# Forming the remainders of double-precision weights on GpSimd instead of TensorE, in an attention and gated-MLP kernel

## The chip, the cores and the metric

The kernel runs on one core of a Trainium2 chip. The core has TensorE (PE in the profile, with its weight loads as PEld), VectorE (DVE), ScalarE (ACT), GpSimd (POOL) and SyncE (SP), which here issues all DMAs. TensorE's results land in PSUM, a memory of eight banks of 128 x 512 float32. The metric is the device time of one execution in microseconds (us), as the median of several runs on the chip.

## The reference

Eight batches, eight heads, 576 tokens, heads of 64. The attention keeps only the scores within `tau` of a row's maximum. Its output, with the heads side by side (512 wide), goes through a gated MLP with a residual.

```python
def _attn_ref(q, k, v, tau):
    scores = scale * np.matmul(q, k.transpose(0, 1, 3, 2))
    thresh = np.max(scores, axis=-1, keepdims=True) - tau
    scores = np.where(scores >= thresh, scores, -1000000000.0)
    scores = scores - np.max(scores, axis=-1, keepdims=True)
    attn = np.exp(scores)
    attn = attn / (np.sum(attn, axis=-1, keepdims=True) + 1e-09)
    return np.matmul(attn, v)

def _moe_ref(x, w_in, g_ln, w_sg, b_sg, w_out):
    h = gelu_tanh(x @ w_in)                              # 512 -> 1024
    u, v = (h[..., :d_ff // 2], h[..., d_ff // 2:])
    v_n = (v - mean(v)) / np.sqrt(var(v) + 1e-06) * g_ln
    v_s = np.einsum('ts,bsd->btd', w_sg, v_n) + b_sg[None, :, None]
    return x + (u * v_s) @ w_out
```

`w_in` (512 x 1024) and `w_out` (512 x 512) arrive in double precision, all else in float32.

## The kernel before

**Two streams of work.** The attention works on 32 pairs of heads, n = 0 to 31, four to a batch. Each pair has nine score tiles of 128 x 576: TensorE forms the scores (L525, L537 for n < 4; L545 after that), DVE takes their maximum (L554), GpSimd a threshold from it (L560, one column), ACT the exponential (L581), and DVE selects, multiplies and sums (L588). For n < 4 the scores are float32 products and the selected tiles are transposed on TensorE (L250) before the product with the values (L727). From n = 4 on, queries and keys are split into two float32r parts (high and low, so that a float32 product becomes two or three float32r products), and DVE turns 32 x 32 blocks (L603) for many small products with the values (L741). The MLP of a batch (`moe`, its products in groups of four at L839) begins when its four pairs are done. Its operands are float32r pairs too: `xh`, `xl` of the attention's output, `wih`, `wil` of `w_in`, `woh`, `wol` of `w_out`.

**The weights** are prepared once, during the first pairs, by `from_double` (L278 to L332). `w_in` makes eight jobs of 128 x 512 ("wide", k = 0 to 7), `w_out` eight jobs of 128 x 256 ("narrow", k = 14 to 21). A job loads the doubles as two 32-bit words, ACT takes the magnitude of the upper word (L293), GpSimd clamps it (L302), and three DVE steps on bits rebuild it as a float32 number in the tile `room` (L308, L310, L312); the last one leaves the scale of the lower word in place of the upper one. The low word is scaled on GpSimd in wide jobs (L297), on ACT in narrow ones (L299). ACT rounds `room` to float32r: that is the high part, `hi` (L329). The low part is `room - hi` plus the low word times its scale. GpSimd forms that last product (L315). TensorE adds the three in a bank of PSUM (L321): `room` times the identity as a float32 product, `hi` times minus the identity (held in the tile `zt1`) and the low word's term times the identity as float32r products. ACT copies the bank into `lo` (L332).

**What sets the order.** Nothing is scheduled at run time and no planner runs at build time. Each step of work is put on a list, and the table `ORDER`, packed into a string, gives the sequence in which the steps are issued (L1150). Each engine takes its own instructions in that sequence and waits by semaphores for what it needs. A second table, `FIRST_BANKS`, gives the PSUM bank of each tile in the order in which tiles are made; a step that needs a bank waits until its last reader is done.

Of the kernel before, what the change touches and what calls it, by code (L numbers as in the profile page):

```python
# [22 lines left out]
P = 128  # L23
# [14 lines left out]
    "a#HG520PDj3M2WklA#e5%+1J($k~O@N~xrA9AqSBxB>SPVn*Vrz^zDWRN$QGk2qp%!V!ZhX?lb<BE3ioOQN;P${tbcM5BN$CM2eT01|a+IE>ty047164cG;d"
    "c9I3<N$8T`l%s<2p}{#~hG-)TM?GowB%E|B%~IA#V@e14F%YZ->7lvOq%k+jKvI%4v_48b&iX~@e?PMp24rlJh9rtuh8$6qBQZGzb0ZO*D$?q}4Fro^NH;?z"
    "j)<mD`;9Ck!e07kWPw_+6p~cVIv{6h!6QyIDm4@(5pcW7nGI5~VKlNE7MAj(Wy&EV3*pp*7A+Z6&Z%$fLMtu6A`_ROaV={n2_%)1g2_(wW9hYw7WU*sHad*A"  # L40
    "b6{J3m^kMwS!bFpwJFj8WfM;t1gTIIMv>-CVj`2%g-XKF+)W%UJ`S0Pp=feeyAxY9kv4odE1sxDftW2tGSNqBBy#vF8mX~}m?f<|d=X9Lz!o%R91_zsA(0Yc"
    "Ff1B<pg81A(HUPHp0<)qh%2SYd|KB%7RM<J&6xJ%W<=Q$EQ~;IC~=HQvuE(ckEP<A>NI_ZN!ukUa0^An=oH#S!6iD3qbQ{$wsbHz$^<b7DND)=nOdz0M?!|O"
    "Lo}E(U94)$0JP-FB#;J68aSFFiHaeJ80?Xq7&&rKEs#X6l`M&GVgpLb1KS}fK}mP!&(NIJ!kJp?g5^pXG2z5lVzrz(gctx*L8==ZQqqD(rYTc)92H$O<2E@b"
    "S+hhr=YUcUoRcbzKq`@=s<o(xCxqy1<D7LWN>Ny%xLa;!?Br$|iK9X|GowQ(XVDlEAtvd}G%!*5*j#0jJ7<ze8{}rWBoCb{5)-L}NH9V{5}Uxv8Im+il%{Bw"
    "(*kdi{gvIE(~e~>Z6HN6_sXV@Dup;ne6fY8iHR&#xO44i<s(&_S(+bm`an`=?c^DmiDb^#hTM#pnsl}i(U4ivl=u@*IaPx#5x9@Thp9znM14iGh-1p>LLiNf"
    "+$@qvaubbelBOp0mO^r722a_sGfvmcri&bzS)pQ3Gt-T5AW?7+BE!Qm7c8<_&axtR<bmi;`{^D{GGxiq_zaU6(dd*3O^nhaaY?I$Dkr|oiZYV3ZtBG`DqO2>"
    "1X{4rjM$rzBG9BcDM`YeFr;Ha9Fdt}P${LmmTv`irS7dC6%5h&pAcgw%2&dmVQ4fu8dN{IS)xy(QvIDDEmTo6_sZ7=V$e)Fvjo91k%CYKne0vr8WG7YtSp#B"
    "EknhGk~nclpad98ITf7^1d_^*4U#h=$AS@TDKUn^wWjIBqJvMQmlBuinaxlODFZrAh-5Ff2=u~)VY-{8$wSJ+LM$wDR#c>V1Wu|JX$TOqFqYI=aHiNYMu?6z"
    "$4NuNNeLh}U7X@L#bpzNl_}29f&}Wx-XM~UsP$VC$<5sV^TEkd!CXmlE!#uF4zUVGEwxK429KYBENs-V4=G=KA+RJjoS?v2h<+Bfp%=_8+Z&QFjgOs(A9f<%"
    "IAaSjqmM*D+(|)512Lvc7D2`jBthC|p)@5X0)`L>3LP-w)RHG{C)nhkhNjZDC?!~&TOy98LBdjQ1ewIfA;^RC<C&$5&xkQZ)R5Yfpo~1Wk&r1-PSVIi+$iz?"  # L50
    ")9TcRdeb`sNBt=n>5$?{xziAoBx6m%7>qO`l&;0843(V<&17T@sR>m|ut<>+6N?(qCaNnbTzW6nlZ3-e2{T5G`V&IV4K>MEvXZu8&TSWgK#Z8cbfHnGGeWPH"
    "Xv=fUBlpT59-O=L*1v8zSHo9ZT0iw#uhKV=^TU&CL2vywZ2jBHD{MHf_0Ke~PA~3%1#G3|{N3Qe(HkGPe?8yaeDl5D3nuXivp2%BM!8L}xao&qP$paz>IJ0`"
    "na4+E@`)L7kmra>m-FtX_&fF}g+-^*d+Jh*m-wuxim+@MA6yVsp?CAHjMNpkF*d^7|BRLGgU)w_CxOqt*ru+q+6@k+%;4cb!q}|(mqu-HzZ2T>AXI_u!F=h2"
    "!?rLRYUpv<A@g%@w&{lFIn;OjUE~F!R`-}QK60D9IB4)COWeJ%(qd&K^3I1u^#RMk6Wv`3M;s19<sChq)c35f6D{7Zjb{08lY*XV+tgYu?W!HfO{KF&JcW8c"
    "ZINHGFAiDeX>-jP{KQ)ACsP^fQ0%k1isq@+_J1`Q^F(cd`!h|KLS={hLHGK}YtO3M^(q!ZFLY}N5JC@y+^t;xElfGvzgp&UdHkCNcX@Z-f9uN`zNLExbkZN1"
    "u|GDrI-#(p0|;dyyspaoz?*Fk{Rrn(n%zlfU(X)PH)x~JhQO0%2<xo9q0`n?M?-PkuklZlv@d=1wt^~EM>ku};3`+E?CJ9$p9<Tas1Z4DKpITn$-f5R5mY8R"
    "8ay2xc8}*>;m(8cma-;3!398`0s2Ap-ts+3_X~vM?>wG)w=(I(-(!+Ik>8q00^-~5NOV{g*AiXpl)m+Lhl^wBn#GgG!4qD=--@#Q=`l1cbz(zkE!Nn~%lJ*7"
# [1104 lines left out]
```

## Time and profile before

| | us |
|---|---|
| median of three runs | 848.71 |
| lowest, highest | 846.18, 850.71 |
| the profiled execution | 849.72 |
| its span in the trace | 847.9 |
| PE, PEld busy | 823.4, 739.8 |
| DVE, ACT, POOL busy | 679.0, 603.8, 584.8 |

The profile is of one execution. Its span runs from the first to the last instruction; 1.8 us of the execution's time lie around it. The granted clock of TensorE was 0.993 of full speed on the mean. A busy time is the union of an engine's instructions, and those of PE are modelled from their starts, so a busy PE is not a full PE.

### The profile page before, as it was taken

How to read it: one execution, taken by the hardware profiler on the slowest of the kernel's cores; microseconds unless marked ns; L12 is line 12 of the kernel's file. 1: busy time of each engine (PE TensorE's matmuls, PEld its weight loads, DVE VectorE, ACT ScalarE, POOL GpSimd, SP SyncE). 2: the span in 40 equal slices, each digit the busy share in tenths (PEclk: the TensorE clock that was granted, in tenths of full speed). 3: DMA queues.
4: the chain of work that ended last, by engine and by line, in shares of the span. 5: the costliest groups of instructions: out<-in, count | busy, mean ns of one | idle time of the engine just before them, and what ended most of it. 6: DMA issues, size and time to landing. Idle time of an engine off the chain costs nothing.

```text
span 847.9 us, 30583 instructions
## 1 busy us (share of the span) xinstructions
PE 823.4 (97%) x12590; PEld 739.8 (87%) x12590; DVE 679.0 (80%) x1288; ACT 603.8 (71%) x1097; POOL 584.8 (69%) x966
## 2 busy tenths in 40 slices
PE   8999999999999999999999999999999999999998
PEld 5666799888889979998899988999899998899898
DVE  7998978888799978978988899789888997876110
ACT  6999987646876769765798468876796767764342
POOL 5975667575766678755777677865797568656676
PEclk9999999999999999999999999999999999999999
DMA  6645245656356665564565575466556555433001
GB/s 229 216 124 158 76 115 148 180 166 168 101 162 189 196 171 152 149 168 137 171 167 151 159 216 147 119 187 188 167 157 188 171 164 152 125 102 87 29 15 56
DMA packets 80189, 125.57 MB, mean 148 GB/s; under 512 B 13745, under 2 KB 36273, under 8 KB 80050
## 3 DMA queue, kind: packets, MB, share of 16 engines
q1 hardware_dynamic: 80050, 123.62, 50.8%
q8 instruction: 99, 1.62, 0.8%
q14 instruction: 40, 0.33, 0.1%
HBM read 70.55 MB, written 9.90 MB: 95 GB/s over the span
## 4 chain that ended last, share of the span: by engine, by line
PE 70%; DVE 7%; DMA 6%; ACT 6%; POOL 4%; issue 4%; SPq 2%; POOLq 0%; DVEq 0%; ACTq 0%
PE all_banks L839 40%; PE all_banks L545 13%; PE all_banks L741 13%; DVE p L588 3%; ACT L1154 2%; ACT p L581 1%; DMA qst<-qhi 1%; DVE turned L603 1%; DVE maxima_of L554 1%; PE all_banks L727 1%; DMA ir<-ld 1%; PE all_banks L525 1%; PE all_banks L250 1%; DMA ks<-khi 1%; DMA w<-in_w_in 1%
## 5 line engine op out<-in xcount | busy, mean ns | idle before, releaser
L581 ACT ACTIVATE p<-all_banks,maxima_of 128x576 f32<-128x576 f32 x256 | 183.4, 737 | 79.2 <-DVE maxima_of L554 70.7
L588 DVE SCALAR_TENSOR_TENSOR p<-all_banks,maxima_of,p 128x576 f32<-128x576 f32 x256 | 201.7, 806 | 35.6 <-ACT p L581 20.7
L554 DVE TENSOR_REDUCE maxima_of<-all_banks 128x1 f32<-128x576 f32 x288 | 206.3, 742 | 26.9 <-PE all_banks L545 21.0
L545 PE MATMUL all_banks<-ks,qst 128*128 128x288 f32 x560 | 154.4, 309 | 8.3 <-DVE p L588 3.6
L603 DVE STREAM_TRANSPOSE turned<-p 128x1152 f32<-128x1152 f32 x112 | 152.0, 1364 | 12.0 <-PE all_banks L741 10.8
L741 PE MATMUL all_banks<-turned,v 32*64 32x144 f32 x8064 | 146.2, 286 | 6.6 <-issue 4.8
L741 PEld LDWEIGHTS all_banks<-turned,v 32*64 32x64 f32 x8064 | 127.3, 130 | 20.2 <-issue 15.6
L545 PE MATMUL all_banks<-klz,qst 128*128 128x288 f32 x448 | 124.3, 296 | 0.0
L545 PEld LDWEIGHTS all_banks<-ks,qst 128*128 128x128 f32 x560 | 101.8, 188 | 23.3 <-DVE p L588 10.2
L560 POOL TENSOR_TENSOR maxima_of<-columns,maxima_of 128x1 f32<-128x1 f32 x288 | 53.5, 193 | 86.7 <-DVE maxima_of L554 79.5
L839 PE MATMUL all_banks<-wsh,z 128*128 128x288 f32 (+2 forms) x512 | 112.8, 299 | 0.0
L1154 ACT ACT_TABLE_LOAD x83 | 106.5, 1283 | 1.5
L839 PEld LDWEIGHTS all_banks<-wsh,z 128*128 128x128 f32 x512 | 85.9, 191 | 1.4 <-issue 1.0
L545 PEld LDWEIGHTS all_banks<-klz,qst 128*128 128x128 f32 x448 | 84.6, 189 | 0.5
L839 PE MATMUL all_banks<-gh,wol 128*128 128x288 f32 (+2 forms) x256 | 75.2, 297 | 0.0
L839 PE MATMUL all_banks<-gh,woh 128*128 128x288 f32 (+2 forms) x256 | 75.1, 296 | 0.1
L839 PE MATMUL all_banks<-wsl,z 128*128 128x288 f32 (+2 forms) x256 | 75.1, 298 | 0.0
L839 PE MATMUL all_banks<-xl,wih 128*128 128x288 f32 (+2 forms) x256 | 74.5, 295 | 0.0
L839 PE MATMUL all_banks<-xh,wih 128*128 128x288 f32 (+2 forms) x256 | 74.2, 295 | 0.0
L839 PE MATMUL all_banks<-xh,wil 128*128 128x288 f32 (+2 forms) x256 | 73.8, 295 | 0.0
L839 PE MATMUL all_banks<-gl,woh 128*128 128x288 f32 (+1 forms) x240 | 70.2, 295 | 0.3 <-POOL gl L1013 0.3
L839 PE MATMUL all_banks<-wih,xh 128*128 128x512 f32 x160 | 63.5, 400 | 0.0
(150 smaller groups left out, 1873.5 us busy)
## 6 DMA issues: line engine op xcount, KB each, us to landing
v<-in_vR SPq DMA_DIRECT2D x112, 288.0 KB, 3.9
ks<-khi SPq DMA_DIRECT2D x112, 144.0 KB, 2.8
rq<-in_qT SPq DMA_DIRECT2D x28, 320.0 KB, 4.1
qst<-qhi SPq DMA_DIRECT2D x56, 160.0 KB, 3.5
qst<-rq SPq DMA_DIRECT2D x56, 160.0 KB, 3.2
rk<-in_kT SPq DMA_DIRECT2D x28, 288.0 KB, 3.6
klz<-kl SPq DMA_DIRECT2D x56, 144.0 KB, 2.6
ir<-ld SPq DMA_DIRECT2D x56, 144.0 KB, 4.1
```

The source lines that it names most:

```text
L250: nc.tensor.transpose(out, x, ident_r.bitcast(F32))
L525: nc.tensor.matmul(st["s", h, i][:, a, 0:HALF], st["q"][rows, qo:qo + P], st["k"][rows, lo:lo + HALF], start=True, stop=True)
L545: nc.tensor.matmul(sc[:, a, 0:HALF], w, x, start=(j == 0), stop=(j == len(terms) - 1))
L554: nc.vector.tensor_reduce(nmax, st["s", h, i][:, :, 0:HALF], AX.XY, ALU.max, negate=True)
L560: nc.gpsimd.tensor_tensor(thr, toff, st["nm", h, i], ALU.subtract)
L581: nc.scalar.activation(target(h, i), st["s", h, i][:, :, 0:HALF], AF.Exp, bias=st["nm", h, i])
L588: nc.vector.scalar_tensor_tensor(dst, st["s", h, i][:, :, 0:HALF], st["thr", h, i], dst, ALU.is_ge, ALU.mult, accum_out=st["l"][:, c:c + 1])
L603: nc.vector.transpose(out, st["p", i].rearrange("p (h k x) -> p k h x", h=2, x=Q))
L727: nc.tensor.matmul(acc[h * D:(h + 1) * D, 0:w], st["v"][:, o:o + D], unit(h, a)[:, kt, 0:w] if kt < NM else tail_unit(a)[:, 0:w], start=(k ...
L741: nc.tensor.matmul(st["accs"][g // 2][hs, g % 2, 0:W], st["v"][rows, o:o + D], st["turned"][rows, k, h * W:(h + 1) * W], start=(k == 0), s ...
L839: nc.tensor.matmul(st["acc"], *term(j), start=(j == 0), stop=(j == n - 1))
L1154: tables[kind]()
```

## The change

`remainder` now has two products in place of three, and runs in wide jobs alone. A new step, `less`, has GpSimd subtract `hi` from `room`. In wide jobs the difference goes to a tile of its own, `rem`, in float32r, and TensorE adds `rem` and the low word's term, each times the identity as a float32r product. In narrow jobs the difference replaces `room`, the low word's product replaces the low word, and a third GpSimd step, `total`, adds the two into `lo`: no product on TensorE, no bank and no copy by ACT are left there. The tile `rem` takes turns in four buffers that `xh` and `xl` of the pairs n = 2 and n = 3 use later. `ORDER` and `FIRST_BANKS` are replaced whole. All line numbers from L40 on move: the scores of L545 become L562, the MLP's products of L839 become L856, and so on.

```diff
 ORDER = (
-    "c-n1P30zcF)PLtOZ{7?u0}QC3?4Tfvptxq>hUS)Nrj=SQh?-k!i&k1$xm0SYNv^n?TDj$txuX~=iVGm1Ae#%a4lv9<bHBU10l)9}Ilk@QbN=Ul{`cJb?t|kv"
+    "c-m!n2V7Iv`~E#4HwlCg!XC0gMgj;ps)AVes2y5I)z&(2&)QboT6fjfI#F9!9d%o+TJ@{ejVM|LMTYDUSt2ugpWhib;Q#agB;0$?d*1WB&-=XZIZ0p`NMHDZ"
...
         def rest(out):
             nc.gpsimd.tensor_tensor(out, t["low"].bitcast(F32), t["up"].bitcast(F32), ALU.mult)
 
+        def less():
+            if wide:
+                t["rem"] = xpool.tile([P, (S, KW)[k % 2]], F32R, tag=("xl3", "xh3", "xl2", "xh2")[k % 4], name=f"rem{k}")[:, 0:w]
+            else:
+                t["rem"] = t["room"]
+            nc.gpsimd.tensor_tensor(t["rem"], t["room"], hi, ALU.subtract)
+
+        def total():
+            nc.gpsimd.tensor_tensor(lo, t["low"].bitcast(F32), t["rem"], ALU.add)
+
         def remainder():
             t["acc"] = bank(f"w{k}_lo")[:, 0:w]
-            one = ident_r.bitcast(F32)
-            for j, (a, x) in enumerate(((one, t["room"]), (minus_r, hi), (ident_r, lo))):
-                nc.tensor.matmul(t["acc"], a, x, start=(j == 0), stop=(j == 2))
+            for j, x in enumerate((t["rem"], lo)):
+                nc.tensor.matmul(t["acc"], ident_r, x, start=(j == 0), stop=(j == 1))
...
         put("w_hi", time, lambda: nc.scalar.activation(hi, t["room"], AF.Copy))
-        put("w_mul", time, lambda: rest(lo))
-        put("w_pe", time, remainder)
-        put("w_low", time, lambda: nc.scalar.activation(lo, t["acc"], AF.Copy))
+        if wide:
+            put("w_rem", time, less)
+            put("w_mul", time, lambda: rest(lo))
+            put("w_pe", time, remainder)
+            put("w_low", time, lambda: nc.scalar.activation(lo, t["acc"], AF.Copy))
+        else:
+            put("w_rem", time, less)
+            put("w_mul", time, lambda: rest(t["low"].bitcast(F32)))
+            put("w_sum", time, total)
```

The first place is GpSimd's queue among the tiles of the first pair, around the first two wide jobs. `wil` is the low word's term, `w` the raw words, `maxima_of` the thresholds of the attention. Before:

```order
L302 TENSOR_SCALAR room_260<-room_260 128x512
L315 TENSOR_TENSOR wil_116<-w_167 128x512
L560 TENSOR_TENSOR maxima_of<-columns,maxima_of 128x1 x2
L297 TENSOR_SCALAR w_175<-w_175 128x512
L315 TENSOR_TENSOR wil_115<-w_169 128x512
L560 TENSOR_TENSOR maxima_of<-columns,maxima_of 128x1
```

The same place now, on the same engine (L304, L317 and L577 are the former L302, L315 and L560; L324 is the new subtraction, L381 the former L364):

```order
L304 TENSOR_SCALAR room_241<-room_241 128x512
L324 TENSOR_TENSOR rem_261<-room_204,wih_112 128x512
L317 TENSOR_TENSOR wil_116<-w_164 128x512
L577 TENSOR_TENSOR maxima_of<-columns,maxima_of 128x1 x2
L317 TENSOR_TENSOR wil_115<-w_166 128x512
L577 TENSOR_TENSOR maxima_of<-columns,maxima_of 128x1
L324 TENSOR_TENSOR rem_300<-room_220,wih_111 128x512
L381 TENSOR_TENSOR wsl_130<-w_172,wsh_126 128x576
L304 TENSOR_SCALAR room_319<-room_319 128x512
L577 TENSOR_TENSOR maxima_of<-columns,maxima_of 128x1
```

Two subtractions stand between the thresholds, one of them ahead of two thresholds at once.

The second place is TensorE's queue in the same pair, around the first wide job. Before:

```order
L727 MATMUL all_banks<-pt_0_242,pt_1_173 64x256 x10
L250 MATMUL all_banks<-ident_r,p_2_278 128x128 x4
L321 MATMUL all_banks<-room_204,ident_r 128x512
L321 MATMUL all_banks<-wih_112,zt_101 128x512
L321 MATMUL all_banks<-wil_116,ident_r 128x512
L525 MATMUL all_banks<-rk_163,rq_154 128x288 x4
```

And now (L744, L252, L332 and L542 are the former L727, L250, L321 and L525):

```order
L744 MATMUL all_banks<-pt_0_228,pt_1_170 64x256 x10
L542 MATMUL all_banks<-rk_158,rq_155 128x288 x4
L332 MATMUL all_banks<-rem_300,ident_r 128x512
L332 MATMUL all_banks<-wil_115,ident_r 128x512
L252 MATMUL all_banks<-ident_r,p_2_277 128x128 x4
```

The float32 product (`room` with the identity) is gone, and the scores of the next tile now stand ahead of the job.

The third place is TensorE's queue where the first batch's MLP runs beside pair n = 4, at the last two narrow jobs. Before:

```order
L839 MATMUL all_banks<-wil_117,xh_1101 128x512
L321 MATMUL all_banks<-room_1023,ident_r 128x256
L321 MATMUL all_banks<-woh_121,zt_101 128x256
L321 MATMUL all_banks<-wol_125,ident_r 128x256
L741 MATMUL all_banks<-turned_1231,v_4_1209 64x144 x72
L839 MATMUL all_banks<-xh_913,wil_116 128x288
L839 MATMUL all_banks<-xh_1101,wih_113 128x288
L839 MATMUL all_banks<-xl_1112,wih_113 128x288
L839 MATMUL all_banks<-xh_1101,wil_117 128x288
L321 MATMUL all_banks<-room_1056,ident_r 128x256
L321 MATMUL all_banks<-woh_120,zt_101 128x256
L321 MATMUL all_banks<-wol_124,ident_r 128x256
```

And now:

```order
L856 MATMUL all_banks<-wil_117,xh_1089 128x288
L758 MATMUL all_banks<-turned_1234,v_4_1072 64x144 x72
L856 MATMUL all_banks<-xh_891,wil_116 128x288
L856 MATMUL all_banks<-xh_1089,wih_113 128x288
L856 MATMUL all_banks<-xl_1100,wih_113 128x288
L856 MATMUL all_banks<-xh_1089,wil_117 128x288
L562 MATMUL all_banks<-ks_0_1256,qst_137 128x288
```

The narrow jobs' products have left the queue, and the scores of pair n = 5 follow the MLP's products directly.

Counted over the two whole sequences: TensorE's instructions fall by 32 (48 products at L321 before, 16 at L332 now), GpSimd's rise by 24, DVE's stay the same. ACT loses 8 copies (L332 before, narrow jobs) and gains two loads of its function table (83 at L1154 before, 85 now) with a one-column operation each. Of the 2,882 products of the MLP, 2,410 stood ahead of the last scores (of n = 31), now 2,432 do; ahead of the last scores of n = 7, 8, 11, 14, 18, 24, 25, 27 and 28 the number is the same in both.

## Rows read from the trace of the kernel before

**Rows 1.** Busy time by stretch: us, PE, PEld, DVE, ACT, POOL, clock, DMA share.

```profile
0.00:84.00 84.00, 78.62 (x487) 49.83 (x487) 73.71 (x163) 72.11 (x158) 58.62 (x118) 0.98 0.58 183
84.00:130.00 46.00, 45.80 (x552) 39.20 (x553) 38.51 (x80) 40.59 (x80) 29.66 (x59) 1.00 0.32 89
130.00:774.00 644.00, 628.77 (x10820) 583.98 (x10820) 553.69 (x1021) 464.77 (x806) 445.94 (x724) 0.99 0.57 160
774.00:847.90 73.90, 70.18 (x736) 66.75 (x734) 13.11 (x27) 26.29 (x56) 50.62 (x67) 0.99 0.12 39
```

**Rows 2.** The page's chain that ended last, whole span, shares by engine.

```profile
PE 70%; DVE 7%; DMA 6%; ACT 6%; POOL 4%; issue 4%; SPq 2%; POOLq 0%; DVEq 0%; ACTq 0%
```

**Rows 3.** VectorE's waits, 10 to 84 us: what was waited for, us, times, longest.

```profile
DVE p L588 <- ACT p L581: 1.5, 3, 1.1
DVE maxima_of L554 <- PE all_banks L525: 1.3, 3, 0.7
DVE p L588 <- POOL wsl L364: 0.9, 1, 0.9
DVE room L308 <- POOL room L302: 0.5, 2, 0.3
DVE p L588 <- POOL maxima_of L560: 0.3, 1, 0.3
DVE sums_of L626 <- POOL sums_of L623: 0.3, 1, 0.3
DVE maxima_of L554 <- PE all_banks L537: 0.2, 1, 0.2
```

**Rows 4.** The chain in order of time: start, us, what.

```profile
27.36 1.33 PE all_banks L321 x4
...
89.50 0.54 PE all_banks L545 x4
...
91.68 5.48 PE all_banks L839 x24
...
103.52 0.67 PE all_banks L321 x4
...
124.75 0.38 ACT wol L332
```

**Rows 5.** GpSimd's groups, 0 to 130 us: busy us, mean ns, idle before.

```profile
L953 POOL TENSOR_TENSOR z<-vv,z 128x512 fp32r<-128x512 f32 x4 | 5.1, 1289 | 1.4 <-ACT z L946 1.4
...
L774 POOL TENSOR_TENSOR xl<-ir,xh 128x256 fp32r<-128x256 f32 x4 | 2.9, 732 | 1.5 <-issue 1.5
```

**Rows 6.** VectorE's groups, 0 to 130 us, same columns.

```profile
L310 DVE SCALAR_TENSOR_TENSOR room<-w,room 128x256 uint32<-128x256 uint32 x8 | 4.0, 503 | 0.1
L308 DVE TENSOR_SCALAR room<-room 128x256 uint32<-128x256 uint32 x8 | 3.7, 472 | 0.5 <-POOL room L302 0.5
```

**Rows 7.** Lines L308 and L310 alone: ns shortest, median, longest.

```profile
L308 DVE TENSOR_SCALAR room<-room x8: 254/292/1483, 59.2 to 94.8; 128x256 uint32<-128x256 uint32 x8
...
L310 DVE SCALAR_TENSOR_TENSOR room<-w,room x8: 407/416/989, 60.8 to 95.7; 128x256 uint32<-128x256 uint32 x8
```

**Rows 8.** All engines in order of time: start, us, instruction.

```profile
59.12 1.40 POOL L438 TENSOR_TENSOR kl<-rk,khi 128x576 fp32r<-128x576 f32 x1
59.19 1.69 DVE L308 TENSOR_SCALAR room<-room 128x256 uint32<-128x256 uint32 x2 [0.23 <-POOL room L302]
```

**Rows 9.** ScalarE's groups, 0 to 130 us: busy us, mean ns.

```profile
L1154 ACT ACT_TABLE_LOAD x6 | 7.7, 1283 | 0.1
...
L332 ACT ACTIVATE wol<-all_banks 128x256 fp32r<-128x256 f32 x8 | 3.0, 380 | 0.6 <-PE all_banks L321 0.5
...
L1154 ACT ACTIVATE spare<-columns 128x1 f32<-128x1 f32 x6 | 1.2, 203 | 0.1
```

**Rows 10.** TensorE's waits, 130 to 774 us.

```profile
PE all_banks L545 <- DVE p L588: 3.6, 5, 1.8
PE all_banks L545 <- DVE pm L588: 3.6, 2, 2.0
```

More of the change, by code (lines that the diff above doesn't have):

```diff
@@ L38 @@
[L38 to L57, printed above, removed]
@@ new lines @@
+    "U^lcF5^QwA=m;KxL6JdZAo?>R1czsl)y6}290n24V|F42YLUbYGNRCEg$U)w!<3ObBF3PVC?rHz1HnWQ4FpUCxrERVlBFa#j@`Mzn2v4Gxz|u^LJkKYH;9SS"
+    "N0cyPz>v%#CX9(O+!}1BOCgqtOrjOY+yMs(FM@{jBhz>hmX-1#nslBASRCxl-5|$-vVmlbaPSP7W*9=snG)zc1v=KzBZO;lE`5vu9f~-P9m1WVix^5vM5eif"
+    "7)}GcoWY)G1@>e(E(FlPa2euSK%B6_kqgP0;cN`Sq}h@o?GH{r19$e}Y8$u&5F<i`pmWO6Cy`M|=x|exa}|@P%0WZNX~`vwue7K{hmNcr4y3Obhq|=P9Wb<j"
+    "(6Na01U4EuBQ!W9q9r0;6qpl`VT7FiWKL+L+0wQnvXiYLGH}(Uu{kK>gK~yO5i~L=b&(O*9tn!?Mp{duk@h#56QY}up$4IW>D&M!BZK^eM$AiyJ+Kdgh4cv<"
@@ new lines @@
+    "(Q+tqB!U+T4V1hHO$iOi(Ex=Eau?##6V=c_WDqj6?~Ovb!|*&bk~kQhc+psxwu2C)9LSrY1IG$T`7wA6aT0MB6rCYKjNC{_vgO8(&nBV>fg}&ye#2wzKrlFf"
+    "cU};u#>HpwB0OXq934X8bWk{k#zr<A9|H@~3L~LQ7j+0rMeqFZcQ7MFY4SuJ;tC04%9U`06r3Uxc^ot_CbbGXs6ot#qalQ}4@fc`8o|O9a414Lhb9Ug61?jK"
+    "9aUlIBS(O%9Y<W~2numbN7|0QqMAS|5vML~T1aH!U^zfY_%O6fI|^k&Qv#*~mw`;D9;CY1l|ZARNkFDZN+wLnMEz-JaD8PYMI^eQ6~x34M--LNWH=DyCZN0t"
+    "F$U5{he|@o*%-3#pn$IK_}+$F6(blszHVWEfr)NH0j3MN_8=4-sne!%d`2)#hk#ruI2}-ekZMEq6PUR671F2zk^@affRuq`Qb6~MNx+x{CL%fg?n!E9LhJ-4"
@@ new lines @@
+    "MnHI=XWW%03=AD~kd2P<1(F5Whunx6=PWeQEU+`apczs^1~(=Oint(D#zf#C#UT_iB@?7ZOaQqt1k^;g5Mc)?GYm=0XqEzDN~G!-Uw~^XU<fGHRRFPpMk3fG"
+    "1&C3IiLRjG3ATWUgc3J#GT@{+4uq3K34tRM0YM>Dh`wYF#brpk2+BnDg``y(hK3^mIBzU683}NDxT8qa4)Hs_)^Hq64jUOj`lcNwpb;I^97C!y$JE5--cb%h"
+    "5HcJLeD?<nedge4T_G)ki8eKrfhJDo1kj9ChMXK!DF;!3nRS%hVeP=fh%6?;^@&4znzq2ykq$#J7_LW5tQqIP@nsoEnuqi&!!?AdQxb-&H+8`VJd10GsF^WA"
+    "YQ%fA<J%Oi6}Ok^Qc`cSl?AlQjEN;}$$j~t`lCNHEt-JJfu>o;Atq7@N5sNAx&enVv$TU5td@g2X(6->kz{FCF;r8o8JW(XnVmlzX^uqKjy8rk0LcwS$6Q!P"
@@ new lines @@
+    "dlMk6I!juamW^dl0xVi)MoUm^k}m=v&1mlYuI>1OiJUo4Grr;xi`J4BN8!v28j)ER-_QaKg>1Mnh&Bv`CCph;6~utS6!2OELRG|BkO;WoL==pReNX{eGbtv="
+    "8EZ}g;%O`lc3}uCW=DXyB@j9=SX^Nm3nL*X90ig<c)(ElBxjBxLxMnz=7?dY;R%CxtSlsgVqsW^8iZa)9?;B@<{lUl8j@+M9YY5AN-hkYB16oO=?q4vVTTHs"
+    "WG5$@6uorn$FPiJM8eV4v~&!eg^uW?un;<O$5kSI$N|#)XiL%r;X9v{&~c8zcN>`LJb^lY#J%%N<{d-F|5)Dr_lpDSoy8qL2|NEq^Z)FWcaA&9e`R3je?FN1"
+    "4+eJpr0aNryyTbi+4}>u+85gvOgU<waCXwEonVDpV1;fb*#G9h|M)34SvP2w7spga7OMwY^Yp2OiM8-;WNvCvBCK_*w5Qzh>mtgQ$=OQJYMIU?FB5s!ilAn}"
@@ new lines @@
+    "KQSqL_~}K1j!)Yc{{97R_gjiKlU4*9d)g|T*j68HjHRL0-N_~HNo0O<eM3aORMTD4?pYFE7HD;^V8fdkp(oF%Z-}ro3H|gwE<U9Ve0OHZT?^mL#FV~v?h>Bm"
+    "|Ng<AvSQdg_@Ch3xv}+6Z!A4CrPaOC9$f2deG%hZ<|QapSkyw`qi=z3W{IR(81%N$U91UqS66#jVXHp8MIy}!=+>rTEW-RY@4?zv0-u5rB@uU{0_t0nEUNG$"
+    "QG)u9Ds0j^Mfu}(B?Xm3{{q7TRcWjIQvAvWtN6TIC2Jn0)|q+DYPQwg*LB-OSKIj^#-LWcSmdV2+qdYz;d`go-L__bX7hPlarK+7g=ONv$B&k<F#J&AGTrm^"
+    "?Mr0${G+vR-7S7Cf}Fd{tik!WO6K^kShe1Hl1ysX3OyG6u|2eTyskb<eI}qjXsGz?2huGITTjn9uL@uXOW0%KdBAJzi9vqsPWNHHI^BU~YG2=4I6BR1hK0X*"
@@ new lines @@
+    "hUbdDeXoxY1RU#gcGi^vcdB<ZLcfnU+3ZeUo2IdQ=J7oqME~hJs|D=H)L7kiHc#F8lUcZUv)ihvVFt^-x`msvKK)v1th%%~%st~{-+kbt4`0@w8L~uGykoCZ"
+    "Ypr&-=<3K{cK-+`mAm{m5FX+~$(LKZ)n|;h1+O?7C>>G0{HMzHM~jwTyc+eCaR*oXybj9g{W=%|srq%0DkSUtSHa!x6b>&60zpMDzOdvMP0fvaDQ%Ov1{jMC"
+    "5w-rB@H}^Evq0=!CH2e~2Zv_Qd!Y<_AejPwO7_njr&oV@OAVZTvw}mP2ifYqo!+!7)aryrr($VHt189lT;V3+gH5yQW<D$wds}P8@;aGG)as^rZHf|^R3W8F"
+    "wwJ;XfdJY}t~#JpJQXGj-bg%+2B+9p0-!aB`HFj??I{InXSep;>5a{1H$#)OLLT{A+-kG9SeIPU*1r-&&(G*?G`cMMT`!c>JRREVG5cDHyU|YtEsCaF@3~IO"
@@ L106 @@
+    "+ds(~`N`2;vwoNP7K{zb>QtEj0)&)MhlJ%B81JL<+qui;N$`>%o(v9_oUij#&ir{(lSu7Nz?f|4<tP6aeC+CdUO^gQW->wd?Aj+)KkJQP)8ovTIvoLjx_t>?"
+    "{KP*wv<Rd"
 )
```

92 lines of the change are left out of this document (44 added, 48 removed).

## The prediction

> **What bounds the kernel now.** I read the busy times by stretch first [rows 1], cut where the chain of waits changes. In the first 84 us, where the four pairs n = 0 to 3 and most of the weights are worked off, all engines are loaded: DVE 73.7 of 84 us, ACT 72.1, GpSimd 58.6, PE 78.6. From 84 to 774 us PE is at 98%, and in the last 73.9 us it works nearly alone. The page's chain puts 70% on PE and 7% on DVE [rows 2], but that is a mean over these stretches. So I looked next at what DVE waits for in the first one [rows 3]: from 10 to 84 us it waits for 5.0 us in all, the sum of seven rows; 1.5 of these end with a product on PE, 2.0 with GpSimd, 1.5 with ACT. DVE's work there (maxima, selections and the weights' bit steps) is the same after the change. This stretch is DVE's, with ACT close behind; PE only looks full. From the chain in order of time [rows 4] I take the prices of PE's work, and that PE leads from the first float32r scores at 89.5 us on.
>
> [...] The trace has 49.8 of 84 us for PEld in the first stretch (59%) and 584.0 of 644 us (91%) from 130 to 774 us [rows 1]. By the matmul row the first stretch would be PE's, and the change would give back everything there; by the PEld row PE has room, and it gives little.
>
> **PE's work removed.** A wide job's products hold the chain for 1.33 us (27.36 in [rows 4]). The two that remain are float32r products of 512 columns, the size of the MLP's at 91.68 us: 5.48 / 24 = 0.228 us each, 0.46 for two. So 0.87 us goes per wide job, 7.0 for eight. A narrow job's 0.67 us (103.52) goes whole. All eight wide jobs and four narrow ones stand ahead of the first float32r scores, four narrow jobs behind them. So PE loses 7.0 + 2.7 = 9.7 us in the first stretch and 4 x 0.67 = 2.7 us in the second, 12.4 in all.
>
> **GpSimd's work added.** The trace has the same kind of operation in both sizes [rows 5]: a subtraction of 128 x 512 into float32r takes 1.29 us, one of 128 x 256 takes 0.73. Eight of the first are 10.3 us, sixteen of the second 11.7. The eight wide jobs and four narrow ones fall into the first stretch: 10.3 + 8 x 0.73 = 16.2 us, so GpSimd goes from 58.6 to 74.8 of 84 us. The other 5.8 us fall into the time after, where it has 29.7 of 46 us: covered.
>
> **The first stretch.** Gain: at most the 5.0 us of DVE's waits; I take the 1.5 that end with PE. Cost, first part: DVE waits 2.0 us for GpSimd beside 58.6 us of its work; in proportion 16.2 more us (28%) add 0.6. The longer waits are for a threshold behind a long operation, and behind a threshold stands DVE's selection, behind that the transposes on PE and the next tile. Second part: the narrow jobs' bit steps on DVE are stretched when GpSimd works. L308 takes 0.254 us at best and 0.472 on the mean [rows 6, 7], L310 0.407 and 0.503: 8 x 0.218 + 8 x 0.096 = 2.5 us now, and 28% more is 0.7. So the stretch changes by -1.5 + 0.6 + 0.7 = -0.2 us. The ends: -5.0 if all waits go, and +16.2 if none of GpSimd's 25.4 idle us can take the new work.
>
> A wait is added where `xh` and `xl` of n = 2 and n = 3 are written: their buffers hold `rem` until PE has read it. Behind such a write ACT and GpSimd would hold all that follows, thresholds too. On ACT the copy that follows the last of these reads (a wide job's `lo`) stands ahead of the first such write (`xh` of n = 2), so nothing new is waited for there, and I take 0; late reads would be part of the 16.2 us.
>
> **84 to 130 us.** PE is busy 45.8 of 46 us, the chain is PE's, and DVE has 38.5 [rows 1]. The four narrow jobs' 2.7 us come out of it. The last one's copy by ACT, 0.38 us, stands in the chain at 124.75 us [rows 4] and goes too. The ends: 0, if what comes next on PE isn't ready, and -3.1. I take -3.1, since here no other engine is as full.
>
> **ACT.** Eight copies of 0.380 us go, 3.0 us; two table loads with their one-column operation come, 2 x (1.283 + 0.203) = 3.0 us [rows 9]. Together I take 0: the copies are counted in the two stretches above, and loads of the MLP's time lie under PE, with ACT at 464.8 of 644 us from 130 us on [rows 1]. Were that cover missing, they would cost 3.0.
>
> **130 us to the end.** The work is the same, piece by piece, and the MLP is as far at each pair as before (equal counts at nine of the pairs). What the new order does to PE's waits there, no row can tell: the largest two are 3.6 us each, both for a selection on DVE [rows 10]. I take 0, and for the range one of them lost or one more gained, 3.6 either way. That 22 more products of the MLP stand ahead of the last scores shortens the tail by 22 x 0.135 = 3.0 us (a float32r product of 288 columns is 0.54 / 4 at 89.50 in [rows 4]), but they are then done where PE is at 98%: 0 as well, -3.0 at best. New banks: where PE is full, a bank that is free earlier gives nothing; in the first stretch it is inside the 5.0 us.
>
> **Sum.** -0.2 - 3.1 + 0 + 0 = -3.3 us. The profiled execution took 849.7 us (a span of 847.9 and 1.8 around it), which gives 846.4. It was 1.0 us above the median of the runs; from 848.7 the same sum gives 845.4, and this is what I predict.
>
> **Rival: all of PE's saving arrives.** If the first stretch is PE's after all, 12.4 us go: 848.7 - 12.4 = 836.3 us. For it: PE's busy row, and 70% of the chain. Against it: DVE's 5.0 us of waits there; to be 9.7 us shorter, the stretch would need DVE at more than it can do, 73.7 us of work in 74.3.
>
> **Rival, slower: GpSimd becomes what DVE waits for.** With 74.8 of 84 us, in strict order and with thresholds between the new operations, GpSimd may run late all through the first stretch. [...] The price: if the wide jobs' subtractions alone lengthen the stretch by their own time, +10.3, less the 1.5 and the 3.1 above, +5.7 us: 854.4. It decides from the point where more than 8.8 of the 16.2 us come out as waits of DVE (4.2 + 3.1 + 1.5). Against it: GpSimd's work beside DVE's now costs only 2.0 + 2.5 us, and the order keeps two narrow jobs' sums back until well behind the first float32r scores. [...]
>
> **Rival: nothing is left over.** DVE and ACT (38.5 and 40.6 of 46 us) set the pace from 84 to 130 us too as soon as PE has less to do, or the new order loses what the products give. Then the time is 848.7 less 0 to 1: about 848.5. For it: ACT at 88% there. Against it: PE at 99.6%, and its chain without a gap up to 124.7 us.
>
> **How the numbers follow.** About 0.5% (4.2 us) is what a measurement of this kernel can tell from no change: below 844.5 is faster, above 852.9 slower. The forecast, 845.4 with a range of its own from 841.8 to 849.0 (3.6 either way), has 0.55; of that some 0.22 lies below 844.5. All of PE's saving has 0.15, all faster. Nothing left over has 0.18, within 0.5% nearly whole. The slower rival has 0.12; 0.09 of it above 852.9, with 0.01 of the one before. Faster 0.38, within 0.5% 0.52, slower 0.10. The range for 8 in 10 goes from 837.5, which leaves out most of the full saving, to 852.5.
>
> **What the changed kernel's profile would show.** PE's first float32r scores stay within 3 us of 89.5 us, and from there to the end the time is 3 us shorter: then the steps are right. DVE's waits for GpSimd from 10 to 84 us are 2 to 4 us; 9 or more mean the slower rival. First scores at 80 us mean the full saving. GpSimd is busy 73 to 77 us in the first 84. [...] What would make it wrong without any of these: another 5 us of PE's waits, gained or lost, between 130 and 774 us.

## The result, and the profile after

The changed kernel takes 855.92 us (median of 9 runs, 851.62 to 861.09), the kernel before 846.41 (9 runs beside them, 844.66 to 850.71): a ratio of 1.0107, 95% interval 1.0077 to 1.0137. It is 9.5 us slower; the prediction was 845.4 with a range to 852.5. The profiled execution took 858.6 us, its span is 856.8. One run of e9 below, of 862.3 us, counts as slow and is left out of e9's figures.

First the busy time by stretch in the changed kernel, to be laid beside [rows 1] (us, then PE, PEld, DVE, ACT, POOL):

```profile
0.00:84.00 84.00, 70.21 (x450) 44.73 (x450) 74.15 (x156) 68.39 (x146) 68.56 (x123) 0.96 0.54 168
84.00:130.00 46.00, 44.05 (x534) 36.02 (x531) 40.88 (x87) 42.20 (x82) 37.84 (x73) 1.00 0.38 109
130.00:774.00 644.00, 623.13 (x10767) 576.45 (x10767) 545.10 (x1002) 462.62 (x802) 444.95 (x720) 1.00 0.56 159
774.00:856.80 82.80, 78.68 (x799) 75.30 (x798) 22.47 (x46) 31.97 (x65) 54.52 (x76) 0.99 0.15 50
```

TensorE's busy time in the first stretch fell by 8.4 us, but DVE got no further: it did 156 instructions there, 163 before, and was busier with them. And from 130 to 774 us TensorE works 5.6 us less, with the same pieces ahead of it: it waits more, as the rows below show.

The waits of DVE, 10 to 84 us, beside [rows 3] (what was waited for, us, times, longest):

```profile
DVE p L605 <- ACT p L598: 1.8, 4, 0.8
DVE p L605 <- POOL maxima_of L577: 1.7, 3, 1.1
DVE maxima_of L571 <- PE all_banks L542: 1.4, 1, 1.4
DVE room L310 <- POOL room L304: 1.2, 3, 0.6
```

The waits of TensorE, 130 to 774 us, beside [rows 10]:

```profile
PE all_banks L758 <- issue: 8.3, 7, 2.2
PE all_banks L562 <- DVE p L605: 4.3, 7, 1.3
PE all_banks L562 <- DVE pm L605: 3.5, 3, 1.7
```

The first of them is the largest and has no releaser: "issue" is time in which TensorE waited for nothing that the profile shows. In the kernel before, the same answer began with this row, which the prediction passed over when it called two waits of 3.6 us the largest:

```profile
PE all_banks L741 <- issue: 4.8, 6, 1.5
```

To see where the time goes I took the start of the last selection of a pair as a milestone, in both traces, and in a second trace of each kernel (e11, e12 below). All are us from the span's start:

```
last selection of pair      3      4      5      7     31   span
before                   87.9  113.5  139.5  188.5  773.9  847.9
before, second trace     87.7  113.3  139.3  187.0  766.7  840.7
after                    90.8  117.5  144.3  187.6  784.1  856.8
after, second trace      90.3  116.6  143.6  186.7  782.3  854.9
after without the
 subtractions (e8)       86.5  112.8  139.2  182.3  780.0  852.1
after, wide as before
 (e10)                   92.0  118.3  145.0  188.0  779.4  852.5
```

The changed kernel is 3 us late at pair 3 and 4.4 to 4.8 at pair 5, has made all of it good at pair 7 (0.9 and 0.3 us ahead), and loses 9.9 and 14.6 us between there and the end, where it does the same work but for four products of the MLP more (three in the second trace; about 0.5 us). The second pair of traces overstates the loss: its spans are 14.3 us apart, the medians 9.5.

**What "issue" is.** This is TensorE's queue in the changed kernel around 515 us (start, us, instruction, idle before it):

```profile
513.78 1.47 PE L758 MATMUL all_banks<-turned,v 32*64 32x144 f32 x72
517.43 0.86 PE L758 MATMUL all_banks<-turned,v 32*64 32x144 f32 x37 [2.18 <-issue]
```

In the middle of a run of small products with the values, where the profile shows no operand that is waited for, TensorE stands still for 2.2 us. In the same time the DMA queues carry one packet of instructions, of 16,384 bytes in the trace (queue, packets, MB, share; 514.6 to 517.6 us):

```profile
q8 instruction: 1, 0.02, 2.3%
```

I then counted TensorE's instructions from the first on, with weight loads and semaphores, in all 14 traces of this study. Between two small products there are 166 gaps of more than 0.25 us, and every one stands ahead of an instruction whose number, counted from 0, is 193 modulo 256. The program runs through 98 or 99 such packets (99 for 25,325 instructions before, 98 for 25,235 after: 256 and 258 each), so I take one packet for a block of 256 instructions, and the place of the gaps for the edge of a block. The gap ends 1.2 to 1.6 us after the end of a packet, in nine cases of ten; that TensorE waits there for the next block is how I read this. A small product costs four instructions, and a run of 72 of them, 288 instructions, is issued in 2.2 us: more than a block. What the stalls go with is how long ago the last edge was (all 14 traces; distance between two edges without the stall itself):

```
us since the last edge   edges   with a stall   us stalled, mean
under 2.5                   98             71               1.17
2.5 to 3.5                 157             78               0.51
3.5 to 4.5                 239             44               0.17
4.5 to 6                   200              8               0.02
over 6                     671              4               0.00
```

About one in four of the closest edges passes without a stall; the traces do not say why.

Edges that lie more than 4.5 us apart are nearly always crossed without a stall (12 stalls at 871 edges). Of the 255 edges that lie less than 3.5 us apart, 149 have one.

Theory 1: the new order of the steady part costs the time. Theory 2: GpSimd's new work does. Theory 3, formed after the first four runs: it is where the block edges fall among the runs of small products.

### The profile page after: what moved, and what is told of

Read it like the earlier page. It is cut to its first block, busy times and chain, and to the rows that moved or that the text cites. A ratio compares the mean times of both kernels' runs of the same rounds, so it can differ in the third digit from the quotient of the medians.

```text
span 856.8 us, 30504 instructions
## 1 busy us (share of the span) xinstructions
PE 816.1 (95%) x12542; PEld 732.5 (85%) x12542; DVE 682.6 (80%) x1288; ACT 605.2 (71%) x1093; POOL 605.9 (71%) x990
## 4 chain that ended last, share of the span: by engine, by line
PE 49%; DVE 6%; POOL 6%; DMA 5%; issue 5%; ACT 3%; SPq 2%; POOLq 0%; DVEq 0%; ACTq 0%
PE all_banks L856 30%; PE all_banks L758 9%; PE all_banks L562 9%; DVE p L605 3%; DVE maxima_of L571 2%; DVE turned L620 1%; DMA rk<-in_kT 1%; DMA ld<-ir 1%; ACT p L598 1%; POOL kl L455 1%; POOL ot L1063 1%; POOL ir L769 1%; POOL z L970 1%; SPq L470 1%; POOL free L1063 1%
## 5 line engine op out<-in xcount | busy, mean ns | idle before, releaser
L562 PE MATMUL all_banks<-ks,qst 128*128 128x288 f32 x560 | 154.7, 310 | 8.4 <-DVE p L605 4.3
L620 DVE STREAM_TRANSPOSE turned<-p 128x1152 f32<-128x1152 f32 x112 | 152.4, 1365 | 10.3 <-PE all_banks L758 9.5
L758 PE MATMUL all_banks<-turned,v 32*64 32x144 f32 x8064 | 149.1, 288 | 12.1 <-issue 9.4
L758 PEld LDWEIGHTS all_banks<-turned,v 32*64 32x64 f32 x8064 | 129.4, 131 | 26.2 <-issue 20.8
L562 PE MATMUL all_banks<-klz,qst 128*128 128x288 f32 x448 | 124.2, 296 | 0.0
L562 PEld LDWEIGHTS all_banks<-ks,qst 128*128 128x128 f32 x560 | 101.7, 188 | 25.9 <-DVE p L605 12.4
L577 POOL TENSOR_TENSOR maxima_of<-columns,maxima_of 128x1 f32<-128x1 f32 x288 | 53.2, 193 | 88.1 <-DVE maxima_of L571 80.0
L856 PE MATMUL all_banks<-wsh,z 128*128 128x288 f32 (+2 forms) x512 | 110.9, 296 | 1.2 <-DVE vt L916 0.5
L856 PEld LDWEIGHTS all_banks<-wsh,z 128*128 128x128 f32 x512 | 84.4, 188 | 2.2 <-DVE vt L916 0.8
L562 PEld LDWEIGHTS all_banks<-klz,qst 128*128 128x128 f32 x448 | 84.4, 188 | 0.7 <-DMA klz<-kl 0.3
L856 PE MATMUL all_banks<-gh,woh 128*128 128x288 f32 (+2 forms) x256 | 75.5, 297 | 0.0
L856 PE MATMUL all_banks<-wsl,z 128*128 128x288 f32 (+2 forms) x256 | 74.7, 295 | 0.0
L856 PE MATMUL all_banks<-gh,wol 128*128 128x288 f32 (+2 forms) x256 | 74.7, 295 | 0.0
L856 PE MATMUL all_banks<-xh,wih 128*128 128x288 f32 (+2 forms) x256 | 74.3, 298 | 0.2 <-DVE p L605 0.2
L856 PE MATMUL all_banks<-xl,wih 128*128 128x288 f32 (+2 forms) x256 | 74.0, 295 | 0.0
L856 PE MATMUL all_banks<-xh,wil 128*128 128x288 f32 (+2 forms) x256 | 73.6, 295 | 0.0
L856 PE MATMUL all_banks<-gl,woh 128*128 128x288 f32 (+1 forms) x240 | 70.8, 296 | 0.0
L769 POOL TENSOR_TENSOR ir<-v,ir 128x576 f32<-128x576 f32 x28 | 40.0, 1430 | 39.7 <-ACT v L765 12.0
```

What stands on the lines that cost most here:

```text
L562: nc.tensor.matmul(sc[:, a, 0:HALF], w, x, start=(j == 0), stop=(j == len(terms) - 1))
L577: nc.gpsimd.tensor_tensor(thr, toff, st["nm", h, i], ALU.subtract)
L620: nc.vector.transpose(out, st["p", i].rearrange("p (h k x) -> p k h x", h=2, x=Q))
L758: nc.tensor.matmul(st["accs"][g // 2][hs, g % 2, 0:W], st["v"][rows, o:o + D], st["turned"][rows, k, h * W:(h + 1) * W], start=(k == 0), s ...
L769: nc.gpsimd.tensor_tensor(st["ir"], st["v"][:, 0:S], st["ir"], ALU.mult)
L856: nc.tensor.matmul(st["acc"], *term(j), start=(j == 0), stop=(j == n - 1))
```

## The experiments

The stalls at edges (number, us) of all kernels, whatever the product behind the edge, and the span without them:

```
kernel                          median us    span   stalls      span less stalls
before                              846.4   847.9    9   7.7    840.2
e12 before, second trace                -   840.7    6   4.7    836.0
e9  before, moved by 16             851.1   843.7   11   7.8    835.9
e5  before, moved by 76             877.4   876.0   21  29.7    846.3
after                               855.9   856.8   10  12.4    844.4
e11 after, second trace                 -   854.9   13  13.6    841.3
e6  after, moved by 148             870.8   867.9   28  31.7    836.2
e8  after, no subtractions          852.3   852.1   13  11.9    840.2
e10 after, wide as before           854.9   852.5   13  14.3    838.2
e3  new order to pair 8, then old   868.1   870.5   20  25.9    844.6
e7  e3, moved by 104                854.6   851.2   14  12.5    838.7
e2  old arithmetic, new order       868.6   866.0   17  20.6    845.4
e4  old order to pair 8, then new   880.2   877.3   13  15.5    861.8
e1  new arithmetic, old order       893.7   891.1   18  26.3    864.8
```

The last column is no clean price of the rest. The kernel before has 835.9 to 846.3 us there at its three places in the stream, the changed kernel 836.2 to 844.4 at its two, so beyond the stalls these traces do not tell the two apart.

### e1 to e4: arithmetic and order apart

The tables `ORDER` and `FIRST_BANKS` were written anew for each. In e1 a job's steps stand like this:

```diff
  w_hi   k
+ w_rem  k      GpSimd: room - hi
  w_mul  k
- w_pe   k      narrow jobs only, with w_low
+ w_sum  k      narrow jobs only
```

Expected of e1: 

> The changed kernel's arithmetic (remainders subtracted on GpSimd, two products for a wide block, none for a narrow one) put into the order and the banks of the kernel before: each new subtraction stands where GpSimd's product stood, each narrow sum where TensorE's products stood. Theory 1 (the new order of the steady part, pairs 14 to 28, costs the time; the arithmetic is worth -3 to +1): 843 to 848 us, that is 0 to 3 us under the kernel before. Theory 2 (16 us more of GpSimd's work in the first 84 us costs the time, wherever it stands): 850 to 858.

Expected of e2: 

> The arithmetic of the kernel before (three products in every block, a copy back by ScalarE) put into the changed kernel's order and banks; rooms of the wide blocks 4 to 7 get buffers of their own, as this order asks. Theory 1 (the order costs it): 853 to 860 us. Theory 2 (GpSimd's added work costs it): 844 to 849.

Expected of e3: 

> The changed kernel's arithmetic; its own order and banks up to the 74th selection (pair 8, about 200 us), and from there on the order and banks of the kernel before. Theory 1: the early loss of 3 to 5 us is already made good at pair 7, so 843 to 849 us. Theory 2 (the early part of the new version, with GpSimd's work, sets it): 853 to 858.

Expected of e4: 

> The converse: the changed kernel's arithmetic in the order and banks of the kernel before up to the 74th selection, and from there on the changed kernel's order and banks. Theory 1: the whole loss comes behind pair 14, so 853 to 859 us. Theory 2: within 2 us of what the arithmetic alone does in the old order.

Measured, as ratios to before: e1 1.0543 (1.0510 to 1.0577), e2 1.0264 (1.0221 to 1.0307), e3 1.0262 (1.0232 to 1.0291), e4 1.0410 (1.0372 to 1.0449). Both theories missed all four; every mixture is slower than either kernel. (In e2 the two latest narrow blocks multiply by a tile that the MLP has overwritten by then, so their low parts come out wrong; the work is the same.)

Two things came of it. In e1 and e4 the early part is late: pair 4's last selection starts at 134.6 and 132.4 us, 21.1 and 18.9 after before. GpSimd's queue was not made for the new steps there. Its own waits in e1, 10 to 84 us, and what DVE then waits for:

```profile
POOL rem L322 <- DMA wt<-bias_hi: 4.3, 1, 4.3
```

```profile
DVE p L603 <- POOL maxima_of L575: 6.7, 8, 2.0
DVE pm L603 <- POOL maxima_of L575: 5.3, 1, 5.3
```

A subtraction waits 4.3 us for its buffer, and a selection on DVE waits 5.3 us for the threshold behind it: the queue, taken in the order of the table, passed its wait on. The other thing is e3. Up to pair 7 it is the changed kernel (188.4 us), behind pair 8 it has the order of the kernel before, and yet it takes 21.4 us more than that kernel. The page's group of small products in e3 (busy, mean ns, idle before) said where to look:

```profile
L757 PE MATMUL all_banks<-turned,v 32*64 32x144 f32 x8064 | 152.5, 288 | 22.3 <-issue 20.8
```

The same group in the kernel before:

```profile
L741 PE MATMUL all_banks<-turned,v 32*64 32x144 f32 x8064 | 146.2, 286 | 6.6 <-issue 4.8
```

The order is the same, but the trace holds 87 instructions of TensorE fewer (25238 against 25325), nearly all of them ahead of pair 8, so every block edge falls elsewhere.

### e5 to e7, e9: TensorE's instructions moved, nothing else

```diff
-   nc.tensor.matmul(x[:, 0:2 * P], pm[:, 0:P], pm[:, 0:2 * P], ...)          # some of the 4 warm-up products
+   for j in range(21):                                                       # 41 in e6, 30 in e7, 4 in e9
+       nc.tensor.matmul(x[j % 2 * D:j % 2 * D + D, 0:16], pm[0:Q, 0:D], pm[0:Q, 0:16], ...)
```

In e9 no warm-up product was taken away.

Expected of e5: 

> The kernel before, nothing changed but TensorE's instruction count ahead of everything: two of the four warm-up products are replaced by 21 tiny ones, so that all later TensorE instructions move by 76 places in the stream. Theory 3 (TensorE reads its instructions in blocks of 256; it stands still at every block's edge that follows the last edge by less than about 3.5 us, which happens in the runs of small products of values; where the edges fall decides): the stalls grow from 8 us to about 26, so 861 to 869 us. Rival (the order of the work and the waits for other engines set it, the edges nothing): 845 to 849.

Expected of e6: 

> The changed kernel with all its TensorE instructions moved by 148 places in the stream (four warm-up products replaced by 41 tiny ones). Theory 3: the stalls at block edges grow from 12 us to about 30, so 870 to 879 us. Rival (the edges are nothing): 854 to 858.

Expected of e7: 

> The kernel of e3 (new order to pair 8, then the old one; 868.1 us) with all its TensorE instructions moved by 104 places, which brings the old part of its order nearly to where it lay in the kernel before. Theory 3: the stalls at block edges fall from 26 us to 6 to 8, so 847 to 853 us. Rival (e3 lost by the mixed order and banks): 866 to 870.

Measured: e5 877.4 us, 1.0350 (1.0314 to 1.0386); e6 870.8, 1.0290 (1.0260 to 1.0320); e7 854.6, 1.0099 (1.0067 to 1.0131). Only e6 came into the range of theory 3; e5 lies 8 us above its range and e7 2 us. But the rival is out three times: the same work in the same order moves by +31.1, +14.9 and -13.5 us when TensorE's stream is moved by 76, 148 and 104 places, and the stalls move by +22.0, +19.3 and -13.4. The changed warm-up is not what does it: at pair 3 e5 is 2.9 us late, e6 1.0, and e7 0.2 early. The row of small products in e5:

```profile
L744 PE MATMUL all_banks<-turned,v 32*64 32x144 f32 x8064 | 153.5, 290 | 21.8 <-issue 20.3
```

and in e7:

```profile
L760 PE MATMUL all_banks<-turned,v 32*64 32x144 f32 x8064 | 146.1, 286 | 5.9 <-issue 3.9
```

The sizes are rougher than the theory. e5 lost 9 us more than its stalls, of which 2.9 us stand at pair 3 already (90.8 us), since its tiny products delay the first scores (the first 16 products of the scores begin at 6.43 us, in the kernel before at 5.39). Most of the rest goes with the clock. In e5 TensorE stood still for 2.3 us at an edge until 710.4 us, and from 711.5 to 714.9 us its granted clock was 0.5 of full speed instead of 1.0. From 130 us to 12 us before the end, the 14 traces hold 28 such stretches at half the clock, 26 of them 3.4 us and two 6.8 us long. 27 begin during an idle time of TensorE of 1.5 to 3.3 us, or within 2.1 us of its end, and 20 of these idle times are stalls at an edge. By the steps between products, against the same steps at the full clock, 3.4 us at half of it cost about 1.5 us (an estimate from e3, e5 and e8; in the kernel before, where such a stretch begins at 300.7 us, a step between products of 288 columns is 0.24 us from 300.9 us on and 0.13 at 297 us). e5 has 23.9 us of them, the kernel before 6.8: about 7.5 us more lost. e6 lost 4 us less than its stalls; in it the gaps between an MLP product and the score behind it, from pair 7 to the end, are 2.3 us in all for 10.8 in the changed kernel (steps of over 0.25 us, from start to start), perhaps since DVE goes on while TensorE stands, which no run shows.

Expected of e9: 

> The kernel before with four tiny products behind its warm-up, which move all later TensorE instructions by 16 places. Theory 3: worked out from the trace of before (every pair of block edges less than 3.4 us apart costs what is missing), the stalls fall from 7.8 to 3.7 us, the least of all shifts, and the four products cost up to 0.5 us: 842 to 844 us, a little faster than the kernel before. Rival (edges so well placed cost nothing any more): 846 to 847.

Measured: 851.1 us (11 runs, 845.5 to 856.1), 1.0053 (1.0026 to 1.0079). A miss for the theory and for the rival: its stalls did not shrink (7.8 us), and its trace is of the shortest execution, 845.5 us, so it does not show what the longer ones lost; that stays open. Distances between edges tell where many stalls will be, not a matter of 4 us.

### e8 and e10: GpSimd's part

```diff
         def less():
             if wide:
-                t["rem"] = xpool.tile(...)
+                t["rem"] = hi
+                return
-            else:
-                t["rem"] = t["room"]
-            nc.gpsimd.tensor_tensor(t["rem"], t["room"], hi, ALU.subtract)
+            t["rem"] = t["room"]
+            nc.gpsimd.tensor_tensor(t["rem"][:, 0:1], t["room"][:, 0:1], hi[:, 0:1], ALU.subtract)
```

Expected of e8: 

> The changed kernel without GpSimd's new work: the wide blocks' subtraction is left out (the product takes the high part instead of the remainder) and the narrow blocks' is cut to one column, so the weights' low parts lack the remainder; order, banks and TensorE's instructions stay. Theory 2 (GpSimd's 16 us in the first 84 cost 3 to 5 us there, by thresholds and words that come late): the first pairs 3 to 5 us earlier, 851 to 853 us. Rival (the new order of the first stretch, not the work, costs it): 855 to 857, first pairs as they were.

Measured: 852.3 us (10 runs), 1.0061 (1.0033 to 1.0089), 3.6 under the changed kernel; pair 3 4.3 us earlier, pair 4 4.7, pair 7 5.3. Theory 2 holds in its size. The eight wide subtractions in the changed kernel, and the narrow ones up to 130 us:

```profile
L324 POOL TENSOR_TENSOR rem<-room,wih 128x512 fp32r<-128x512 f32 x8 | 10.6, 1322 | 0.6 <-ACT wih L340 0.4
L324 POOL TENSOR_TENSOR room<-room,woh 128x256 f32<-128x256 f32 x8 | 6.0, 756 | 0.0
```

What they do to DVE shows in the third bit step of the wide jobs (10 to 90 us; busy, mean ns). Changed kernel:

```profile
L314 DVE TENSOR_SCALAR w<-room 128x512 uint32<-128x512 uint32 x8 | 7.7, 960 | 0.0
```

e8:

```profile
L314 DVE TENSOR_SCALAR w<-room 128x512 uint32<-128x512 uint32 x8 | 5.4, 672 | 0.0
```

the kernel before:

```profile
L312 DVE TENSOR_SCALAR w<-room 128x512 uint32<-128x512 uint32 x8 | 4.2, 531 | 0.1
```

and one of them in order of time, in the changed kernel:

```profile
62.73 1.47 POOL L324 TENSOR_TENSOR rem<-room,wih 128x512 fp32r<-128x512 f32 x1
62.97 1.51 DVE L314 TENSOR_SCALAR w<-room 128x512 uint32<-128x512 uint32 x1
```

The step begins beside the subtraction and ends 0.28 us after it, 1.51 us for what takes 0.41 to 0.43 in six of the eight cases of the kernel before. Six of the eight wide steps of the changed kernel begin beside a GpSimd operation of 0.61 to 1.55 us, and each ends 0.28 to 0.29 us after that operation and takes 0.77 to 1.82 us; the other two, with a threshold alone beside them, take 0.42 and 0.43 us. Why the step ends so late is not shown. Eight steps at 0.960 instead of 0.672 us are 2.3 us, and DVE's waits from 10 to 84 us are 6.1 us against 4.2 in e8, 1.9 more: together 4.2 of the 4.3 us at pair 3.

e10 keeps the new order and the narrow jobs' new form and gives the wide jobs their three products back:

```diff
             if wide:
-                t["rem"] = xpool.tile(...)
+                return
...
-            for j, x in enumerate((t["rem"], lo)):
-                nc.tensor.matmul(t["acc"], ident_r, x, ...)
+            for j, (a, x) in enumerate(((one, t["room"]), (minus_r, hi), (ident_r, lo))):
+                nc.tensor.matmul(t["acc"], a, x, ...)
```

Expected of e10: 

> Half of the change in the new order and banks: the narrow blocks as in the changed kernel (GpSimd alone), the wide ones with three products as before, without the subtraction on GpSimd (rooms of wide blocks 4 to 7 in buffers of their own). Theory 2: the wide subtractions take 10.6 of the 16 us of GpSimd's added work, and with them VectorE's third bit step goes back from 0.96 us to about 0.6, so pair 4 comes 3 to 4 us earlier than in the changed kernel; TensorE's stream is 32 instructions longer from there on, which by theory 3 costs 1 to 2 us: 852 to 855 us in all. Rival (the narrow blocks' sums cost it): pair 4 as in the changed kernel, 856 to 858.

Measured: 854.9 us, 1.0094 (1.0061 to 1.0126): the total as expected, the reason not. The bit step fell to 0.590 us, yet pair 4 is not earlier (118.3 us). DVE's waits in e10, 10 to 84 us:

```profile
DVE p L605 <- ACT p L598: 3.1, 4, 1.9
DVE maxima_of L571 <- PE all_banks L542: 2.7, 4, 1.4
```

The scores come later. All subtractions on GpSimd cost 4.7 us at pair 4 (after against e8). The wide half of the change alone, products against subtractions, is e10 against after: 118.3 and 117.5 us, an exchange at nearly even terms. (e10 is 5.5 us behind e8, but it has the narrow subtractions too, so this is not the price of the wide products.)

### e11, e12: both kernels once more

Expected of e11: 

> The changed kernel unaltered, for a second trace. From pair 7 to the end its first trace holds 11.0 us of stalls at block edges against 5.9 of the kernel before, and 4.8 us more than before that are no such stall. If that remainder belongs to the new order it stands here again (3 to 6 us against the second trace of before); if it is chance it is anywhere between -3 and +5. The stalls: 10 to 14 us in all.

Expected of e12: 

> The kernel before unaltered, for a second trace: 844 to 849 us, stalls at block edges 6 to 10 us in all, 650 to 656 us from pair 7 to the end without them if its first trace is typical.

Measured: 856.7 and 842.4 us, one execution each. e12 lies below all three of its ranges. Stalls 13.6 and 4.7 us, so those of before vary by 3 us from one execution to the next. From pair 7 to the end without them: 656.1 us after, 648.9 before, 7.2 apart where the first traces had 4.8 (658.1 and 653.4). Part of the difference is the clock: from pair 7 on, the run's end left out, before has two stretches at half the clock (from 235.8 and 300.7 us) and its second trace none, after has one in each (from 592.0 us in the first). At 1.5 us a stretch the remainder is 6.3 and 5.7 us, so it was no chance. But it is no fixed price of the new order either: without stalls the same part takes 647.4 us in e6 and 651.3 in e10, in that order at other places in the stream.

## Why the prediction was wrong

**First stretch, -0.2 us: mis-sized, 2.6 to 3.0 us late at pair 3.** The gain was right: without the subtractions pair 3 comes 1.4 us earlier than before, for 1.5 forecast. The cost was not: 4.3 us instead of 0.6 + 0.7. Scaling DVE's waits with GpSimd's busy time gave 0.6; from e8 to the changed kernel those for GpSimd grew by 1.2 (1.7 to 2.9) and all by 1.9; the stretching was reckoned for the narrow jobs' steps alone ([rows 8] shows it once), and the wide jobs' third step, where most of it came, had no row in the prediction. The slower rival looked for the cost at GpSimd too. Its price, 10.3 us for the wide subtractions' whole time, no run shows, and its deciding point was 8.8 of GpSimd's 16.2; all subtractions cost 4.7 at pair 4. Its time, 854.4, is near the result for another reason.

**84 to 130 us, -3.1: right in size, but later.** From pair 3 to pair 7 the changed kernel needs 96.7 and 96.4 us, the kernel before 100.7 and 99.4, with 1.8 and 0 us of stalls in before and 1.3 and 1.5 in after. So 3.9 and 2.9 us came, 3.5 and 4.4 without the stalls. All of it came between pairs 5 and 7, behind the stretch; up to pair 5 another 1.8 us were lost. About 1 us of it is work put elsewhere: eight transposes now stand ahead of pair 3, and four MLP products (three in the second trace) behind pair 7.

**ACT, 0: no run tests it, and nothing speaks against it.** 85 table loads instead of 83, and ACT is busy 605.2 us for 603.8.

**130 us to the end, 0 with 3.6 either way: this step failed.** From pair 7 on the loss is 9.9 us, in the second traces 14.6. Of it 5.1 and 7.4 are stalls at block edges, which no term of the prediction held. It reasoned that the work was the same, piece by piece, and looked at waits with a name. That 48 matmul records less on TensorE (12542 for 12590) and another order move each edge of a block was not considered, nor that the edges of the kernel before may fall well: moved by 16 and by 76 places it stalls for 7.8 and 29.7 us, at its own place for 7.7. A further 3.4 us in each pair of traces are gaps between an MLP product and the score behind it (7.4 to 10.8 us, 6.6 to 10.0 in the second traces; steps of over 0.25 us, from start to start, 6 of them before and 12 and 11 after), about the 3.6 that were allowed. The waits for DVE of [rows 10] are the smaller part of that: 7.8 us now for 7.2. 1.4 and 3.8 us are left; with the stretches at half the clock set off (1.5 us the one way, 1.5 the other) they come to about 3 and 2, and 0.5 of that is the MLP products put behind pair 7. Whether the new order brings these gaps or TensorE's head start does is open: e10 has the same order with 5.3 us of them and e6, with its many stalls, 2.3. Open too is how the changed kernel would do with few stalls, since no run moved it to such a place. The last 73.9 us became 1.3 us shorter, for at best 3.0.

**The signs.** The first float32r scores came within 3 us of 89.5, as said:

```profile
90.89 0.40 PE L562 MATMUL all_banks<-ks,qst 128*128 128x288 f32 x1
```

DVE's waits for GpSimd were 2.9 us (2 to 4 said), the new subtractions 1.32 and 0.76 us (1.29 and 0.73 said). GpSimd was busy 68.6 of 84 us, not 73 to 77: three narrow subtractions and two sums fell in instead of four of each, about 2 us, and some 4 us of its former work slid behind 84 us. From the first scores to the end it was not 3 us shorter but 7.3 longer: that was the sign that the last paragraph had kept for a loss between 130 and 774 us.

## What to carry to other kernels

Idle time put down to "issue" on a full engine can be a wait too, as the 8.3 us of TensorE were here: count that engine's instructions and see whether the gaps stand at one place of a fixed block (193 of 256 in all 166 here) before calling the rest of the program unchanged. Where a run of very short instructions is longer than a block, as here (288 instructions for 256), any edit that changes the number or order of TensorE's instructions moves all edges behind it, so a comparison should be made at two or three offsets: the kernel before took 846, 851 and 877 us at three. What moves to GpSimd can be paid twice, as here, in VectorE's waits (1.9 us more) and in its bit steps that ran beside it (2.3 us), and the row to look at is the one whose mean is already far over its shortest (0.531 us for 0.411 here).

## What the runs showed of the hardware

TensorE's small products were issued at 8 ns an instruction (288 in 2.2 us). Where two block edges lay less than 3.5 us apart it stood still at 149 of 255 (1.17 us an edge on the mean under 2.5 us, 0.51 from 2.5 to 3.5); at 4.5 us and more almost nothing was left (12 of 871). A stall ended 1.2 to 1.6 us after a packet's end in nine cases of ten. Of 28 stretches at a granted clock of half of full speed, 27 began during or just behind an idle time of TensorE of 1.5 to 3.3 us, 20 of these a stall at an edge. Moving an unchanged program by 76 instructions cost 31 us of 846. Two executions of one kernel differed by 3 us in such stalls, 7.7 and 4.7.
